# Last 192 tokens of each batch through the second MoE layer with weights and tokens swapped, and the result turned in 32 by 32 blocks on VectorE

## The chip, the cores and the metric

One core of a Trainium2 chip. The metric is the device time of one execution in microseconds (us). Each kernel was run several times beside runs of the kernel before on the same chip, and compared with them. A run of one kernel counts as slow when it takes over 1.5% longer than the fastest run of the same kernel, else as fast. One execution of each was profiled, on a clock that starts with the profile's span; that span is about 2 us shorter than the time of the run. Engines in the profile: PE (TensorE matmul), PEld (weight load), ACT (ScalarE), DVE (VectorE), POOL (GpSimd), SP (SyncE, which here only issues DMAs; "SPq" and "ACTq" lines are issues of DMAs). The granted clock is the share of the full TensorE clock that the profile's clock record shows. Head and tail are the stretches before PE is in full flow (the first 60 us) and after its last matmul; an eviction copies a result out of PSUM, the memory that PE writes.

## The reference

Eight batches of 2496 tokens with 256 channels. A Fourier mixing layer comes first; then each batch goes through one of eight experts, chosen per batch:

```python
def _moe_ref(x, w_gate, w1, w2):          # x: [8, 2496, 256] from the Fourier layer
    ...
    for e in range(E):
        mask = e_idx == e
        h = np.maximum(x[mask] @ w1[e], 0.0)                      # 256 -> 1024
        out[mask] = gate_w[mask, None, None] * (h @ w2[e])        # 1024 -> 256
```

## The kernel before

The kernel declares operations with an estimated cost, dependencies and a virtual time. A greedy list scheduler then emits them once, so that the order on every engine is static.

The chunks of a batch, and the second layer: hidden activations `hs` stand as weights (128 tokens), w2 streams 256 columns, and the result has tokens on partitions, so that a store writes whole rows of 1 KB.

```python
NCH = [(0, 512), (512, 512), (1024, 512), (1536, 512), (2048, 448)]
# ...
for sp in range(2):                                  # two pairs of token tiles per chunk
    for q in range(4):
        def mm(_, ...):
            i = q // 2
            s0 = min((2 * sp + i) * P, nl - P)       # 0, 128, 256 and 320: the last two overlap
            for ft in range(4 * (q % 2), 4 * (q % 2) + 4):
                nc.tensor.matmul(oc["p"][:, i, :], cell["hs"][:, ft, s0 : s0 + P],
                                 w2s_t[b][:, ft, :], start=(ft == 0), stop=(ft == E - 1))
    # ... eviction times the gate, on ACT or DVE, 128 x 512 fp32
    def st(_, ...):
        if 256 * sp + 256 <= nl:
            nc.sync.dma_start(out=out[b, r0 : r0 + 256, :].rearrange("(i p) c -> p i c", p=P), in_=ost)
        else:                                        # last pair: 128 rows and 64 rows
            nc.sync.dma_start(out=out[b, r0 : r0 + P, :], in_=ost[:, 0, :])
            nc.sync.dma_start(out=out[b, r0 + P : ns + nl, :], in_=ost[64:P, 1, :])
```

With 448 tokens the fourth tile computes 64 tokens a second time.

The same sync queue carries the two trips to DRAM of the Fourier layer of the batches that follow. Their names are used throughout:

```python
# A -> fwd ("fwd stores"), four per batch, then fwd -> XB ("XB loads"), five per batch, which feed PE
nc.sync.dma_start(out=fwd_t[b][6 * g0 : 6 * g1].rearrange("(g q) k c -> (q k) g c", q=6),
                  in_=A_t[b][:, g0:g1, :])
nc.sync.dma_start(out=XB_t[b][:, 4 * q : 4 * q + 4], in_=fwd_t[b][:, 4 * q : 4 * q + 4])
# V -> scr ("scratch stores"), five per batch, then scr -> V2 ("V loads"; the profile calls both tiles V)
nc.sync.dma_start(out=scr_t[b][i][:, k : k + 4, :], in_=hc["V"])
nc.sync.dma_start(out=V2_t[b][rows, g0:g1, :], in_=scr[0:126].rearrange("(g q) k c -> (q k) g c", q=6)[:, g0:g1, :])
```

## Time and profile before

| | kernel before |
|---|---|
| time, median (range of 3 runs) | 435.06 us (434.79 to 435.96) |
| span of the profile | 433.1 us |
| PE busy, granted clock | 97%, 1.0 |
| PE's share of the chain that ended last | 89% |
| end of PE, from there to the end of the span | 429.4 us, 3.7 us |

From the page of the kernel before: busy time of the engines (us, share of the span, instructions) and the chain that ended last, by engine and by line.

```profile
PE 419.6 (97%) x3553; PEld 312.2 (72%) x3553; DVE 300.8 (69%) x614; ACT 333.0 (77%) x643; POOL 35.4 (8%) x57
...
PE 89%; DMA 5%; ACT 3%; POOL 1%; SPq 1%; issue 0%; DVE 0%; ACTq 0%; POOLq 0%
PE ps L1300 30%; PE ps L1337 29%; PE ps L895 9%; DMA xin<-in_x_dram 4%; PE ps L1040 4%; PE ps L527 3%; PE ps L793 3%; PE ps L857 3%; PE ps L1219 2%; PE ps L699 2%; ACT hs L1312 1%; DMA tf<-d_tf 1%; PE ps L613 1%; PE ps L732 0%; POOL xin L321 0%
```

L1300 is the first MoE layer and L1337 the second. No load of XB or V is in the chain. The busy share alone would not prove a PE bound, because matmuls overlap in the pipeline; so I also took the distance between the starts of successive matmuls and subtracted the columns' time. Starts are 56 ns apart at 128 columns, 109 at 256, 189 at 448 and 216 at 512, which is columns/2.4 + 2.5 ns. The columns sum to 411.3 us and PE loses 13.6 us to waits, of which 12.1 us in the first 60 us. This sum, "PE's lost time", is used below.

The timeline of the sync queue in one period (start us, duration us, instruction, and how many in a row were merged):

```profile
101.92 0.33 SPq L967 DMA_DIRECT2D V<-scr  x1
102.30 0.74 SPq L972 DMA_DIRECT2D V<-scr  x1
103.54 0.40 SPq L1364 DMA_DIRECT2D out_dram<-ost  x1
104.38 0.36 SPq L1369 DMA_DIRECT2D out_dram<-ost  x1
104.80 0.51 SPq L1371 DMA_DIRECT2D out_dram<-ost  x1
109.77 0.35 SPq L815 DMA_DIRECT2D fwd<-A  x1
...
122.18 2.24 SPq L834 DMA_DIRECT2D XB<-fwd  x5
```

L1369 and L1371 are the two stores that the change replaces. After them the queue is idle for more than 4 us, until the first fwd store at 109.77.

The end of the kernel before, same columns; in brackets idle time before an instruction and what ended it:

```profile
427.30 2.13 PE L1337 MATMUL ps<-w2s,hs 128*128 128x256 f16 x17
...
429.47 0.47 ACT L1378 ACTIVATE ost<-ps,gbc 64x256 f32<-64x256 f32 x1 [1.12 <-PE ps L1337]
429.97 0.55 ACTq L1381 DMA_DIRECT2D out_dram<-ost  x1
```

One eviction and one DMA follow PE's last matmul.

### The profile page before, as it was taken

What the parts mean: (1) busy time and instruction counts of PE and PEld (TensorE: products, weight loads), DVE (VectorE), ACT (ScalarE), POOL (GpSimd) and SP (SyncE); (2) the same over time, 40 slices, a digit from 0 to 9 for tenths busy, and PEclk for the clock granted to TensorE, in tenths of its full rate; (3) what the DMA queues carried; (4) which work ended last, traced back from release to release, by engine and by line L of the source; (5) the groups of instructions that cost most, each with busy time, mean ns of one, the idle gap of its engine ahead of it and who ended that gap; (6) DMA issues with size and microseconds to landing.
All of it is one profiled execution on the core that took longest, in us unless ns stands there. A gap on an engine that the chain in (4) does not pass through costs nothing.

```text
span 433.1 us, 9390 instructions
## 1 busy us (share of the span) xinstructions
PE 419.6 (97%) x3553; PEld 312.2 (72%) x3553; DVE 300.8 (69%) x614; ACT 333.0 (77%) x643; POOL 35.4 (8%) x57
## 2 busy tenths in 40 slices
PE   5888999999999999999999999999999999999996
PEld 2456567778777877778777877778777787777775
DVE  1488866577977787786977878777877869513561
ACT  3789987688876877678867888678777788678884
POOL 5230100011002000021001100020000010000000
PEclk9999999999999999999999999999999999999999
DMA  8899197999895997879995998959987285521122
GB/s 153 224 181 148 33 248 230 200 174 206 208 280 121 226 197 206 248 140 239 180 243 183 194 205 214 284 103 226 207 215 236 87 160 129 182 88 68 50 99 92
DMA packets 85785, 76.96 MB, mean 178 GB/s; under 512 B 7673, under 2 KB 72695, under 8 KB 85740
## 3 DMA queue, kind: packets, MB, share of 16 engines
q1 hardware_dynamic: 68262, 57.41, 48.3%
q0 software_dynamic: 17216, 18.70, 28.5%
q8 instruction: 28, 0.46, 0.5%
q10 hardware_dynamic: 262, 0.25, 0.2%
q14 instruction: 17, 0.14, 0.1%
HBM read 57.54 MB, written 37.49 MB: 219 GB/s over the span
## 4 chain that ended last, share of the span: by engine, by line
PE 89%; DMA 5%; ACT 3%; POOL 1%; SPq 1%; issue 0%; DVE 0%; ACTq 0%; POOLq 0%
PE ps L1300 30%; PE ps L1337 29%; PE ps L895 9%; DMA xin<-in_x_dram 4%; PE ps L1040 4%; PE ps L527 3%; PE ps L793 3%; PE ps L857 3%; PE ps L1219 2%; PE ps L699 2%; ACT hs L1312 1%; DMA tf<-d_tf 1%; PE ps L613 1%; PE ps L732 0%; POOL xin L321 0%
## 5 line engine op out<-in xcount | busy, mean ns | idle before, releaser
L1312 ACT ACTIVATE hs<-ps 128x512 f16<-128x512 f32 (+1 forms) x293 | 168.2, 594 | 68.6 <-PE ps L1300 64.7
L1300 PE MATMUL ps<-ysb,w1s 128*128 128x512 f16 (+1 forms) x640 | 178.4, 374 | 0.1
L1337 PE MATMUL ps<-w2s,hs 128*128 128x256 f16 x1152 | 162.4, 272 | 0.1
L1337 PEld LDWEIGHTS <-hs 128*128 128x128 f16 x1152 | 110.8, 98 | 42.7 <-issue 0.2
L1300 PEld LDWEIGHTS <-w1s 128*128 128x128 f16 x640 | 68.6, 113 | 18.8 <-issue 0.6
L909 DVE TENSOR_TENSOR tt<-ps,bias 128x512 f16<-128x512 f32 x60 | 38.6, 686 | 24.5 <-PE ps L895 24.5
L937 DVE TENSOR_TENSOR Y<-z,cl 64x512 f16<-64x512 f16 x120 | 50.4, 420 | 2.8
L895 PE MATMUL ps<-w,XT 128*128 128x256 f16 x360 | 49.4, 273 | 0.0
L1354 ACT ACTIVATE ost<-ps,gbc 128x512 f32<-128x512 f32 x65 | 44.8, 689 | 2.3 <-PE ps L1337 2.3
L895 PEld LDWEIGHTS <-XT 128*128 128x128 f16 x360 | 35.2, 98 | 7.7
L918 DVE TENSOR_TENSOR z<-ps,tt 128x512 f16<-128x512 f32 x60 | 38.4, 681 | 0.1
L803 ACT CAST A<-ps 120x512 f16<-120x512 f32 x48 | 29.5, 614 | 7.0 <-PE ps L793 6.6
L1056 DVE CAST ysb<-ps 128x468 f16<-128x468 f32 (+1 forms) x24 | 15.0, 629 | 25.6 <-PE ps L1040 25.5
L1056 ACT CAST ysb<-ps 128x468 f16<-128x468 f32 (+1 forms) x60 | 28.0, 523 | 3.2 <-PE ps L1040 2.6
L865 DVE CAST XT<-ps 128x512 f16<-128x512 f32 x24 | 16.5, 688 | 16.0 <-PE ps L857 16.0
L534 ACT CAST V<-ps 128x512 f16<-128x512 f32 x44 | 25.7, 609 | 0.0
L793 PE MATMUL ps<-xin,wa 117*120 117x512 f16 x66 | 23.1, 380 | 0.4 <-ACT ysb L1013 0.4
L534 DVE CAST V<-ps 128x512 f16<-128x512 f32 x26 | 17.9, 688 | 6.5 <-PE ps L527 5.4
L1040 PE MATMUL ps<-wi,V 120*128 120x117 f16 (+1 forms) x308 | 22.4, 214 | 0.0
L865 ACT CAST XT<-ps 128x512 f16<-128x512 f32 x36 | 22.0, 615 | 0.0
L527 PE MATMUL ps<-Y,ti 128*128 128x256 f16 x140 | 21.8, 272 | 0.0
L1040 PEld LDWEIGHTS <-V 120*128 120x128 f16 x308 | 19.8, 98 | 2.4
(104 smaller groups left out, 415.0 us busy)
## 6 DMA issues: line engine op xcount, KB each, us to landing
out_dram<-ost SPq DMA_DIRECT2D x72, 256.0 KB
xin<-in_x_dram POOLq DMA_DIRECT2D x21, 429.0 KB, 11.3
scr<-V SPq DMA_DIRECT2D x35, 256.0 KB
XB<-fwd SPq DMA_DIRECT2D x30, 256.0 KB
V<-scr SPq DMA_DIRECT2D x14, 504.0 KB
fwd<-A SPq DMA_DIRECT2D x18, 360.0 KB
w1s<-in_moe_w_dram POOLq DMA_DIRECT2D x8, 512.0 KB, 7.1
w2s<-in_moe_w_dram POOLq DMA_DIRECT2D x8, 512.0 KB, 8.9
```

What stands on the lines that cost most here:

```text
L534: COPY[eng](out=hc["V"][:, n * u : n * u + n].rearrange("p i c -> p (i c)"), in_=hc["p", u])
L865: COPY[eng](out=cell["X"][:, ch, :, 0:2].rearrange("p a r i k -> p a i r k"), in_=hc["p"].rearrange("p (a i r k) -> p a i r k", a=2, i=2, ...
L895: nc.tensor.matmul(pm[:, D * a : D * a + D], cell["X"][:, ch, a, t].rearrange("p i k -> p (i k)"), w4[:, ch, t, :], start=(ch == 0), stop= ...
L909: nc.vector.tensor_add(out=cell["tt"][:, r], in0=cell["T", 2].rearrange("p (a c) -> p a c", a=2), in1=bias[:, r].unsqueeze(1).to_broadcast ...
L918: nc.vector.tensor_add(out=cell["z"][:, r], in0=cell["T", 1 - r].rearrange("p (a c) -> p a c", a=2), in1=cell["tt"][:, r])
L937: nc.vector.tensor_sub(out=Y[64 * r : 64 * r + 64, :, i], in0=cell["z"][s, r], in1=cell["cl"][s, r])
L1040: nc.tensor.matmul(pi[:, 117 * i : 117 * i + M], V2[:, g, ch * P : ch * P + P], w)
L1056: COPY[eng](out=yv[:, :, 12 * gb : 12 * gb + 3 * nf].rearrange("p a (g j) -> p a g j", j=3), in_=pi[:, 0 : 117 * nf].rearrange("p (g a j) ...
L1300: nc.tensor.matmul(ph[:, 0:nl], w1v[:, ch, fc // 4, :, fc % 4], ysb_t[b][:, ch, ns : ns + nl], start=(ch == 0), stop=(ch == 1))
L1312: nc.scalar.activation(out=o, in_=i, func=AFT.Relu)
L1337: nc.tensor.matmul(oc["p"][:, i, :], cell["hs"][:, ft, s0 : s0 + P], w2s_t[b][:, ft, :], start=(ft == 0), stop=(ft == E - 1))
L1354: nc.scalar.activation(out=ost, in_=oc["p"], func=AFT.Copy, scale=gbc_t[b])
```

## The change

The intent is to stop computing 64 tokens twice. For the last 192 tokens of each batch w2 stands as the weights and the tokens stream (192 columns), twice for the two halves of 128 channels. Channels are then on partitions, so DVE turns the evicted tile in blocks of 32 by 32. After that each row of 32 channels of a token is contiguous, but the blocks of a token lie on four groups of partitions, so eight stores with pieces of 128 bytes put them in place. In the last batch the list order of the two pairs is reversed.

```diff
-    NCH = [(0, 512), (512, 512), (1024, 512), (1536, 512), (2048, 448)]
+    NCH = [(0, 512, ((0, P), (2 * P, 3 * P))), ... ,          # cut
+           (2048, 448, ((0, P), 256))]
+    def add_turned(b, ns, nl, s0, cell, h_ops, hk, wk, gb_op, v):
+        n = nl - s0                                            # 192
+        for h in range(2):
+            def mm(_, h=h):
+                # cut: one PSUM bank, both halves
+                for ft in range(E):
+                    nc.tensor.matmul(
+                        oc["p"][:, h], w2s_t[b][:, ft, P * h : P * h + P],
+                        cell["hs"][:, ft, s0:nl],
+                        start=(ft == 0), stop=(ft == E - 1))
+        # cut: eviction of 128 x 384 times the gate, on ACT or DVE
+        def tr(_):
+            oc["t"] = ot = opool.tile([P, 2, D], FP32, name="ost")
+            nc.vector.transpose(out=ot..., in_=oc["o"]...)     # cut
+        e = S.op("DVE", 0.5, tr, v, deps=[e], lat=0.6)
+        def st(_):
+            ov = out[b, ns + s0 : ns + nl, :].rearrange(
+                "(t r) (h q c) -> q r h t c", r=32, h=2, c=32)
+            for q in range(4):
+                for h in range(2):
+                    nc.sync.dma_start(
+                        out=ov[q, :, h],
+                        in_=ot[32 * q : 32 * q + 32, n * h : n * h + n].rearrange(
+                            "r (t c) -> r t c", c=32))
+        S.op("SP", 2.4, st, v, deps=[e], dma=1.5)
...
-                v = v0 + PERIOD * (c * 8 + fc) / 44
+                v = v0 + PERIOD * (x + fc * nl / 512) / 44     # x = ns / 64
...
+            if b == B - 1 and c == 4:
+                order = order[::-1]
```

More of the change, by code (lines that the diff above doesn't have):

```diff
@@ L1149, in add_gating @@
         return w, o, wk
-    NCH = [(0, 512), (512, 512), (1024, 512), (1536, 512), (2048, 448)]
+    NCH = [(0, 512, ((0, P), (2 * P, 3 * P))), (512, 512, ((0, P), (2 * P, 3 * P))),
+           (1024, 512, ((0, P), (2 * P, 3 * P))), (1536, 512, ((0, P), (2 * P, 3 * P))),
+           (2048, 448, ((0, P), 256))]
     def add_weight_sums(b, w, wk, v):
@@ L1276, with ev @@
     T_t = {}
+    def add_turned(b, ns, nl, s0, cell, h_ops, hk, wk, gb_op, v):
+        n = nl - s0
+        tag = "o" if b < B - 1 else "h"
+        ok = S.tok(tag, BANKS[tag])
+        oc = {}
+        for h in range(2):
+            def mm(_, h=h):
+                if h == 0:
+                    oc["p"] = bank(tag)[:, 0 : 2 * n].rearrange(
+                        "p (h t) -> p h t", h=2)
+                for ft in range(E):
[3 more added lines that the diff above has]
+                        start=(ft == 0), stop=(ft == E - 1))
+            m = S.mm([n] * E, mm, v, deps=h_ops, after=m if h else None,
+                     allocs=[] if h else [ok])
+            hk.rel.append(m)
+            wk.rel.append(m)
+        def ev(eng):
+            oc["o"] = ost = opool.tile([P, 2, D], FP32, name="ost")
+            o = ost.rearrange("p h c -> p (h c)")[:, 0 : 2 * n].rearrange(
+                "p (h t) -> p h t", h=2)
+            if eng == "ACT":
+                nc.scalar.activation(out=o, in_=oc["p"], func=AFT.Copy,
+                                     scale=gbc_t[b])
+            else:
+                nc.vector.tensor_scalar_mul(out=o, in0=oc["p"],
+                                            scalar1=gbc_t[b])
+        e = S.evac(2 * n, ev, v, deps=[m, gb_op])
+        ok.rel.append(e)
+        def tr(_):
+            oc["t"] = ot = opool.tile([P, 2, D], FP32, name="ost")
+            nc.vector.transpose(
+                out=ot.rearrange("p h c -> p (h c)")[:, 0 : 2 * n],
+                in_=oc["o"].rearrange("p h c -> p (h c)")[:, 0 : 2 * n])
+        e = S.op("DVE", 0.5, tr, v, deps=[e], lat=0.6)
+        def st(_):
+            ot = oc["t"].rearrange("p h c -> p (h c)")[:, 0 : 2 * n]
+            ov = out[b, ns + s0 : ns + nl, :].rearrange(
[7 more added lines that the diff above has]
+        S.op("SP", 2.4, st, v, deps=[e], dma=1.5)
     def add_moe(b, y_ops, yk, gate):
@@ L1282, in add_moe @@
             t_op = add_weight_sums(b, w, wk, v0 - 0.05 * PERIOD)
-        for c, (ns, nl) in enumerate(NCH):
+        for c, (ns, nl, tiles) in enumerate(NCH):
+            x = ns / 64
             hk = S.tok("hs", BUFS["hs"])
@@ L1320, in add_moe @@
                 continue
-            for sp in range(2):
+            order = [*enumerate(tiles)]
+            if b == B - 1 and c == 4:
+                order = order[::-1]
+            for sp, tile_s in order:
+                if isinstance(tile_s, int):
+                    add_turned(b, ns, nl, tile_s, cell, h_ops, hk, wk, gb_op,
+                               v0 + PERIOD * (x + 6 * nl / 512 + 4 * sp) / 44)
+                    continue
                 tago = "o" if b < B - 1 else "h"
                 ok = S.tok(tago, BANKS[tago])
-                last = b == B - 1 and c == 4 and sp == 1
+                last = b == B - 1 and c == 4
                 ok2 = S.tok(tago, BANKS[tago])
@@ L1327, in add_moe, with mm @@
                 for q in range(4):
-                    v = v0 + PERIOD * (c * 8 + 6 + 4 * sp + q) / 44
-                    def mm(_, sp=sp, q=q, nl=nl, cell=cell, oc=oc, tag=tago,
+                    if q // 2 >= len(tile_s):
+                        break
+                    v = v0 + PERIOD * (x + 6 * nl / 512 + 4 * sp + q) / 44
+                    def mm(_, tile_s=tile_s, q=q, cell=cell, oc=oc, tag=tago,
                            last=last):
@@ L1334, in mm @@
                         i = q // 2
-                        s0 = min((2 * sp + i) * P, nl - P)
+                        s0 = tile_s[i]
                         for ft in range(4 * (q % 2), 4 * (q % 2) + 4):
@@ L1362, in st @@
                     r0 = ns + 256 * sp
-                    if 256 * sp + 256 <= nl:
-                        nc.sync.dma_start(
-                            out=out[b, r0 : r0 + 256, :].rearrange(
-                                "(i p) c -> p i c", p=P),
-                            in_=ost)
-                    else:
-                        nc.sync.dma_start(out=out[b, r0 : r0 + P, :],
-                                          in_=ost[:, 0, :])
-                        nc.sync.dma_start(out=out[b, r0 + P : ns + nl, :],
-                                          in_=ost[64:P, 1, :])
+                    nc.sync.dma_start(
+                        out=out[b, r0 : r0 + 256, :].rearrange(
+                            "(i p) c -> p i c", p=P),
+                        in_=ost)
                 def ev_last(_, ns=ns, nl=nl, sp=sp, oc=oc):
@@ L1378, in ev_last @@
                     nc.scalar.activation(
-                        out=ost[64:P, 1], in_=oc["p", 1][64:P, 1],
-                        func=AFT.Copy, scale=gbc_t[b][64:P])
-                    nc.scalar.dma_start(out=out[b, r0 + P : ns + nl, :],
-                                        in_=ost[64:P, 1, :])
+                        out=ost[:, 1], in_=oc["p", 1][:, 1],
+                        func=AFT.Copy, scale=gbc_t[b])
+                    nc.scalar.dma_start(out=out[b, r0 + P : r0 + 2 * P, :],
+                                        in_=ost[:, 1, :])
                 def ev_first(_, ns=ns, sp=sp, oc=oc):
```

## The prediction

> What bounds the kernel now. PE is busy 97% of the 433.1 us span at a granted clock of 1.0 (busy shares, clock row) and holds 89% of the chain that ended last; the only DMA in that chain (5%) is at the start. In the trace, matmuls of one line start 109 ns apart at 256 columns, 56 ns at 128, 189 ns at 448, 216 ns at 512. That is columns/2.4 + about 2.5 ns, as the Trainium skill has it (TensorE: Matmul & The Clock Gate, section "Back-to-back issue gap"); this trace agrees. Weight loads (98 ns each) hide even under 128 columns. So the time is a sum of streamed columns plus head and tail; ACT (77%) and DVE (69%) are second.
>
> What the change does. In the 448-token chunk of each batch, the last two 128-token tiles overlapped by 64 tokens: 16 matmuls x 256 columns. Now w2 stands and 192 tokens stream: 16 x 192 columns, estimate 82.5 ns each. Saved: 16 x (109 - 82.5) = 0.42 us per batch, 3.4 us over 8 batches, all on the PE chain. That is the ceiling of the gain, 0.8%.
>
> Added per batch: an eviction of 384 instead of 512 columns (estimate 0.58 us, between the measured 482 ns at 256 and 689 ns at 512), one DVE transpose of 128x384 fp32 (estimate 0.5 us), and 8 stores of 24 KB in 128-byte pieces in place of two stores (0.36 + 0.49 us of issue). Back-to-back issues of small DMAs take about 0.45 us in the trace (XB loads 0.43, 64-row stores 0.47), so 8 take about 3.5 us on SP. In the middle batches SP waited up to 4.2 us just there for the next A tiles, so this should nearly fit. 1536 pieces of 128 bytes per batch: packets of 256 bytes took 18 ns and of 512 bytes 39 ns on average, so 2 to 4 us of the 16 engines per batch. The Trainium skill (DMA: Bandwidth & Descriptors, "Specifications") says writes below 512 B are read-modify-write; no run shows its cost yet. I allow 0 to 2 us for PE waits from this and from the reshuffled static order.
>
> The tail. The instruction order shows that in the last batch, although the tiles are listed in reverse, the scheduler places the turned matmuls last on PE, the transpose last on DVE and its 8 stores last on SP. Before: PE ends at 429.45, ACT eviction 0.47, one store issue 0.55, end at 433.1: 3.65 us after PE. After: eviction 0.58, transpose 0.5, hand-overs 0.1, 8 issues 3.5, landing and end 2.6 (as before from the end of the issue): about 7.3 us after PE. So the tail costs about 3.6 us, off PE but on the critical path, and eats the 3.4 us.
>
> Sum: 435.06 - 3.4 + 3.6 + about 0.7 for waits and the new order = 436.0 us. Range 433.8 to 439.0. Chances: faster by over 2% 0.01, within 2% 0.95, slower by over 2% 0.04.
>
> What would show it. Turned matmuls start 82 to 83 ns apart; PE's last matmul ends 2.5 to 3.5 us earlier than 429.45; from there to the end 6.5 to 8.5 us, with the transpose and eight store issues last; issues of turned stores 0.4 to 0.5 us each; about 12,000 more packets of 128 bytes; the same granted clock.
>
> What would make it wrong. Store issues costing much less (0.3 us: tail only 2 us longer) or much more; 128-byte writes so slow that they delay scratch trips, with PE waits on XB or V loads; a static order luckier or worse by over 1 us; output buffers held long enough to stall ACT.

## More of the kernel before

PE does not wait for them: this is the group of the matmuls that use XB (count, busy us, mean ns of one, idle us before), and what V loads cost the sync queue (us in total, times, longest).

```profile
L857 PE MATMUL ps<-tf,XB 128*128 128x128 f16 x240 | 18.3, 219 | 0.0
...
SPq L1364 <- DMA V<-scr: 3.7, 5, 0.9
```

## The result

| | before | after |
|---|---|---|
| time, median (range, 4 runs each) | 435.37 us (434.79 to 435.96) | 447.74 us (446.42 to 449.99) |
| ratio, 95% interval | | 1.0289 (1.0243 to 1.0336) |
| span of the profile | 433.1 us | 448.3 us |
| PE busy, granted clock | 97%, 1.0 | 94%, 0.986 |
| time of all columns on PE | 411.3 us | 407.9 us |
| PE's lost time between 100 and 340 us | 0.9 us | 14.4 us |
| from PE's end to the end of the span | 3.7 us | 7.4 us |

A ratio is the mean time of one kernel's fast runs over the mean of the other's in the same rounds, so it is not quite the ratio of the medians. The result is slower by 2.9%, outside the stated range.

From the page after, the same lines as before:

```profile
PE 422.2 (94%) x3553; PEld 311.7 (70%) x3553; DVE 303.1 (68%) x626; ACT 336.7 (75%) x639; POOL 35.1 (8%) x57
...
PE 78%; DMA 12%; ACT 4%; SPq 1%; issue 1%; POOL 1%; DVE 1%; ACTq 0%; POOLq 0%
PE ps L1356 26%; PE ps L1402 23%; PE ps L895 8%; DMA XB<-fwd 5%; DMA xin<-in_x_dram 4%; PE ps L793 3%; PE ps L1040 3%; PE ps L527 3%; PE ps L857 3%; PE ps L1221 3%; DMA scr<-V 2%; PE ps L1292 2%; PE ps L699 2%; ACT hs L1368 1%; DMA tf<-d_tf 1%
```

The chain now leaves PE for XB loads and scratch stores, 7% of the span together. Two lines of the view of waits after (who waited for whom: us in total, times, longest) name the engine that lost the time, and one line of the sync queue's own waits says what held the turned stores (L1327):

```profile
PEld L857 <- DMA XB<-fwd: 10.9, 5, 3.4
...
PE ps L857 <- DMA XB<-fwd: 8.5, 5, 3.0
```

```profile
SPq L1327 <- DMA V<-scr: 21.5, 6, 4.7
```

The turned stores write results that no V load touches, and still they waited for V loads, once in each of six batches. The records of each issue in the trace explain it: this program gives the sync queue's DMAs eight completion semaphores in rotation, and a DMA first waits until the DMA that used its semaphore eight issues earlier has landed. Two V loads and six turned stores use up the eight; the seventh and the eighth turned store must wait for the V loads. The timeline of the sync queue after, in the period shown above:

```profile
106.18 0.34 SPq L972 DMA_DIRECT2D V<-scr  x1
106.62 7.22 SPq L1327 DMA_DIRECT2D out_dram<-ost  x8
113.95 1.45 SPq L815 DMA_DIRECT2D fwd<-A  x1
115.49 0.44 SPq L546 DMA_DIRECT2D scr<-V  x1
116.02 1.42 SPq L815 DMA_DIRECT2D fwd<-A  x1
...
121.16 2.15 SPq L815 DMA_DIRECT2D fwd<-A  x1
...
126.42 2.24 SPq L834 DMA_DIRECT2D XB<-fwd  x5
```

The eight stores hold the queue for 7.2 us, of which 3.4 us is that wait (the view of waits limited to this stretch) and the rest eight issues of 0.44 us (their median). The first fwd store goes out at 113.95, 4.2 us later than before, and the XB loads at 126.42, also 4.2 us later. PE waits at 131.15 and again in each of the four following periods. In one of them the wait was long enough to cost clock as well. The longest wait of the timeline after, and the same kernel's busy times by stretch (stretch, length, engines' busy time, PEclk, DMA share, GB/s):

```profile
184.38 1.03 PE L857 MATMUL ps<-tf,XB 128*128 128x128 f16 x8 [2.96 <-DMA XB<-fwd]
```

```profile
183.00:191.00 8.00, 6.62 (x34) 4.47 (x35) 2.40 (x4) 1.62 (x3) 0.00 (x0) 0.57 0.74 251
```

The clock record has PE at half clock from 183.55 to 190.38 us, 6.8 us. The Trainium skill (TensorE: Matmul & The Clock Gate, "What's actually happening") describes half rate after an idle window of about 3.4 us. Here the wait was 3.0 us on PE and 3.4 us on the weight load, but the record turned to half 0.8 us before it ended, 2.6 us after the last weight load; so the trace agrees that a long wait costs clock, but not on the length. The matmuls that then ran at half clock (256 columns 213 ns apart instead of 109) cost 2.9 us of the 14.4 us. Of the four timed runs, two had a mean granted clock of 0.986 and 0.987 and took 448.3 to 450.0 us; the other two had 0.993 and 0.994 and took 446.4 to 447.1 us. The loss is there without the dip in the clock, so the dip is a consequence and the smaller part.

The turned matmuls and the transpose themselves, from the groups by line and shape (count, busy us, mean ns of one, idle before):

```profile
L1292 PE MATMUL ps<-hs,w2s 128*128 128x192 f16 x128 | 12.9, 246 | 0.0
L1316 DVE STREAM_TRANSPOSE ost<-ost 128x384 f32<-128x384 f32 x8 | 4.6, 578 | 13.4 <-ACT ost L1306 13.4
```

The mean of 246 ns is the length of one pipelined matmul; the starts of the turned matmuls are 82 ns apart. The end of the kernel after:

```profile
439.44 1.48 PE L1292 MATMUL ps<-hs,w2s 128*128 128x192 f16 x16
439.69 0.47 ACT L1437 ACTIVATE ost<-ps,gbc 128x256 f32<-128x256 f32 x1 [2.04 <-PE ps L1402]
...
440.96 0.58 ACT L1306 ACTIVATE ost<-ps,gbc 128x384 f32<-128x384 f32 x1 [0.80 <-PE ps L1292]
441.57 0.58 DVE L1316 STREAM_TRANSPOSE ost<-ost 128x384 f32<-128x384 f32 x1 [2.26 <-ACT ost L1306]
442.18 3.90 SPq L1327 DMA_DIRECT2D out_dram<-ost  x8
```

The sum over both profiles: columns -3.4 us, PE's lost time in the middle +13.5, in the last 90 us +0.6, in the head +0.9 (the head varies by about that much between any two profiles), the tail +3.7: together +15.3 us, against 15.2 us measured between these two spans.

### The profile page after: what moved, and what is told of

Same layout as the page of the kernel before. It is cut to its first block, busy times and chain, and to the rows that moved or that the text cites. A ratio compares the mean times of both kernels' runs of the same rounds, so it can differ in the third digit from the quotient of the medians.

```text
span 448.3 us, 9474 instructions
## 1 busy us (share of the span) xinstructions
PE 422.2 (94%) x3553; PEld 311.7 (70%) x3553; DVE 303.1 (68%) x626; ACT 336.7 (75%) x639; POOL 35.1 (8%) x57
## 4 chain that ended last, share of the span: by engine, by line
PE 78%; DMA 12%; ACT 4%; SPq 1%; issue 1%; POOL 1%; DVE 1%; ACTq 0%; POOLq 0%
PE ps L1356 26%; PE ps L1402 23%; PE ps L895 8%; DMA XB<-fwd 5%; DMA xin<-in_x_dram 4%; PE ps L793 3%; PE ps L1040 3%; PE ps L527 3%; PE ps L857 3%; PE ps L1221 3%; DMA scr<-V 2%; PE ps L1292 2%; PE ps L699 2%; ACT hs L1368 1%; DMA tf<-d_tf 1%
## 5 line engine op out<-in xcount | busy, mean ns | idle before, releaser
L1368 ACT ACTIVATE hs<-ps 128x512 f16<-128x512 f32 (+1 forms) x306 | 175.0, 590 | 70.7 <-PE ps L1356 66.7
L1402 PE MATMUL ps<-w2s,hs 128*128 128x256 f16 x1024 | 147.0, 274 | 0.0
L1402 PEld LDWEIGHTS <-hs 128*128 128x128 f16 x1024 | 99.9, 98 | 41.9 <-issue 2.3
L1419 ACT ACTIVATE ost<-ps,gbc 128x512 f32<-128x512 f32 x52 | 35.6, 685 | 0.9 <-ACT ysb L1056 0.7
L1056 DVE CAST ysb<-ps 128x468 f16<-128x468 f32 (+1 forms) x36 | 21.2, 592 | 20.7 <-PE ps L1040 19.8
L534 ACT CAST V<-ps 128x512 f16<-128x512 f32 x53 | 30.6, 599 | 0.5
L857 PE MATMUL ps<-tf,XB 128*128 128x128 f16 x240 | 19.8, 222 | 8.5 <-DMA XB<-fwd 8.5
L803 ACT CAST A<-ps 120x512 f16<-120x512 f32 x43 | 24.3, 617 | 2.8 <-PE ps L793 2.8
L857 PEld LDWEIGHTS <-XB 128*128 128x128 f16 x240 | 15.8, 99 | 14.0 <-DMA XB<-fwd 10.9
L1056 ACT CAST ysb<-ps 128x468 f16<-128x468 f32 (+1 forms) x48 | 21.9, 529 | 1.8 <-PE ps L1040 1.8
```

Of the source, the lines that this page charges most:

```text
L857: nc.tensor.matmul(px[:, P * i : P * i + P], XB_t[b][:, k1, ch * P : ch * P + P], tf[:, k1, :])
L1056: COPY[eng](out=yv[:, :, 12 * gb : 12 * gb + 3 * nf].rearrange("p a (g j) -> p a g j", j=3), in_=pi[:, 0 : 117 * nf].rearrange("p (g a j) ...
L1368: nc.scalar.activation(out=o, in_=i, func=AFT.Relu)
```

## The experiments

Theory A: the sync queue is held too long by the eight stores (their issues, and the landing wait eight DMAs back), so fwd stores and XB loads come late and PE waits. Theory B: the 1536 pieces of 128 bytes per batch load the DMA engines. Theory C: the rearranged static order costs the time. Later a theory D, that the turned work itself is needed for the loss.

In the first four runs only the emission of the stores was changed, not what the scheduler was told: the order on PE, ACT, DVE and POOL is identical to the changed kernel's (compared instruction by instruction), and on SP identical but for the stores themselves.

### e1_eight_long: eight stores, long pieces

```diff
-  ov = out[b, ns+s0 : ns+nl, :].rearrange("(t r) (h q c) -> q r h t c", r=32, h=2, c=32)
+  ov = out[b, ns+s0 : ns+nl, :].rearrange("n c -> (n c)").rearrange("(q h r e) -> q h r e", q=4, h=2, r=32)
```

> The changed kernel with its 8 turned stores per batch, same bytes, but each writes 32 contiguous pieces of 768 bytes instead of 192 pieces of 128 bytes (the result is wrong on purpose). Order of instructions on all five engines is identical to the changed kernel's. Theory A (the sync queue is held: 8 issues in a row, and issues 7 and 8 wait until the two V loads issued 8 DMAs earlier have landed, so the fwd stores and XB loads behind them come late and PE waits for XB): stays slow, 444 to 449 us. Theory B (1536 pieces of 128 bytes per batch load the DMA engines): falls to 432 to 436 us. Theory C (the rearranged static order itself): 447 us.

Measured: 442.89 us, ratio 1.0173 (1.0136 to 1.0209). Its output is wrong, which doesn't matter for the time. PE's lost time in the middle is still 10.3 us. Most of the loss stays without any short piece, so B is not the main cause. The time is lower than the 444 to 449 us expected for A, though, so short pieces do add to the hold: from the first store to the first fwd store it lasts 7.2 us here and 8.4 us in the changed kernel (means of five periods). By the medians against the kernel before, 8.0 us of the loss of 12.4 us stay and 4.4 us go with the short pieces. The wait of the stores for V loads is as long without them (22.2 us, 7 times).

### e2_one_short and e3_one_long: one store

```diff
-  for q in range(4):
-      for h in range(2):
-          nc.sync.dma_start(...)                       # 8 stores
+  nc.sync.dma_start(out=flat.rearrange("(j p c) -> p j c", p=P, c=32), in_=ot.rearrange("p (j c) -> p j c", c=32))   # e2: 1536 pieces of 128 bytes
+  nc.sync.dma_start(out=flat.rearrange("(p e) -> p e", p=P), in_=ot)                                                # e3: 128 pieces of 1536 bytes
```

> One store per batch of the same bytes in the same 1536 pieces of 128 bytes (wrong result on purpose), same order on all engines otherwise. Theory A: the queue is held for about 0.4 us only; PE no longer waits for XB and the tail shrinks from 7.4 to about 4.5 us: 432 to 435 us. Theory B: stays at 445 to 449 us. Theory C: 447 us.

> One store per batch in 128 pieces of 1536 bytes (wrong result on purpose), same order otherwise. Theories A and B both: about 432 us, that is before minus 3.4 us of PE plus 0.5 us of longer tail. Theory C (order): 445 us or more. The difference of this run to the one-store run with short pieces is the cost of 128-byte pieces alone.

Measured: 434.40 us, ratio 0.9989 (0.9958 to 1.0019), for one store in 128-byte pieces; 433.84 us, ratio 0.9966 (0.9931 to 1.0001), for one store in long pieces. Their outputs are wrong, which doesn't matter for the times. The loss is gone with all the matmuls, transposes and short pieces still in place, so B and C fall as main causes. Between the two runs short pieces cost 0.6 us when the queue is not held, which is not clear of noise (the intervals overlap); the tail in the two profiles is 5.1 us with them and 4.2 us without. C keeps a small part: in both, PE's lost time in the middle is 1.9 us instead of 0.9 and in the last 90 us 1.2 instead of 0.6, with no wait for XB.

### e4_swap: V loads behind the turned stores

```diff
   def rd(_, i=i, k0=k0, k9=k9, g0=g0, g1=g1):        # emits a V load
+      if i == 0 and b >= 2:
+          HOLD.append(lambda: rd_now(...)); return    # first pair of V loads: kept back
...
   # in st(), after the eight turned stores
+  for f in HOLD: f()
+  HOLD.clear()
```

> The changed kernel (right result) with one swap on the sync queue in six batches: the two V loads that stood just ahead of the 8 turned stores now stand just behind them, so no turned store has a V load 8 DMAs ahead of it. Theory A with the landing wait as its main part: the hold falls from about 7.2 to 3.6 us and the time to 436 to 441 us. Theory A with the 8 issues as its main part: 444 us or more. Theories B and C: 447 us.

Measured: 436.41 us, ratio 1.0039 (1.0008 to 1.0070), right result. Eight stores with 128-byte pieces remain; only two DMAs changed places with them, and nearly 11 of the 12.4 us are gone. The timeline of the sync queue of this kernel, in the same period:

```profile
102.57 4.22 SPq L1334 DMA_DIRECT2D out_dram<-ost  x8
107.75 0.31 SPq L974 DMA_DIRECT2D V<-scr  x1
108.11 0.56 SPq L979 DMA_DIRECT2D V<-scr  x1
108.78 0.37 SPq L816 DMA_DIRECT2D fwd<-A  x1
...
122.43 2.24 SPq L835 DMA_DIRECT2D XB<-fwd  x5
```

The hold is 4.2 us instead of 7.2, it starts earlier because the stores no longer stand behind the V loads' own wait for scratch, and the fwd store is on time again. PE ends at 427.0 us, 2.4 us before the kernel before; the tail of 7.3 us takes that back. The swap removes two things at once, the landing wait and the place behind the V loads. Run e5 below tests the second.

### d1_behind and d2_ahead: tiny stores in the kernel before

```diff
+  def small_stores(b):
+      for i in range(6):                                       # 1 KB each, to a DRAM tile of their own
+          nc.sync.dma_start(out=d_i, in_=eye[0:16, 0:32])
   # d1: called just after the first pair of V loads of a batch; d2: just ahead of it
```

> The kernel before, nothing turned, with six tiny stores of 1 KB put on the sync queue just behind each pair of V loads (six batches), so that the seventh and eighth DMA after the loads must wait for them as the last two turned stores did. Order on all other engines identical to the kernel before. Theory A (the landing wait, 8 DMAs back, in the sync queue's order is what costs): 441 to 447 us, with PE waiting for XB loads and sync waits on V loads of about 20 us. Rival (the number of issues in a row, or the 128-byte data): at most 1 us over the control with the stores ahead.

> Control: the same six tiny stores per batch put just ahead of the V loads. Same number of issues. Both theories: 435 to 437 us.

Measured: 435.84 us, ratio 1.0013 (0.9988 to 1.0038), behind; 434.92 us, ratio 0.9998 (0.9976 to 1.0021), ahead. The expectation for the stores behind was a miss. The landing wait did appear (in the view of waits the sync queue waited 24.4 us for V loads, 12.6 and 11.8 us on two lines, against 3.7 us in the kernel before), but PE lost nothing. The timeline says why: the hold began at 103.75 and ended with the first fwd store at 111.05, only 1.3 us later than in the kernel before, since the queue's idle time stood at that place. So the landing wait by itself is harmless at this place. What counts must be how late the fwd stores leave; in the changed kernel the stores also began 3 us later, at 106.6. The sync queue of d1_behind in that period ("idle" is the tile that the tiny stores write):

```profile
103.75 3.02 SPq L492 DMA_DIRECT2D idle<-eye  x6
109.47 0.40 SPq L1371 DMA_DIRECT2D out_dram<-ost  x1
...
111.05 0.57 SPq L820 DMA_DIRECT2D fwd<-A  x1
```

### d3_hold12 and d3_hold20: longer holds in the kernel before

```diff
   nc.sync.dma_start(out=out[b, r0 + P : ns + nl, :], in_=ost[64:P, 1, :])
+  if b < 6: small_stores(b)                                    # 12 or 20 tiny stores
```

> The tiny stores behind the V loads did not slow the kernel before: there the sync queue's hold reached only to 111.05 us (first fwd store of that period, against 109.77 before and 113.95 in the changed kernel), because 4.1 us of idle queue time soaked it up. Theory A in its threshold form: the time is lost only once the hold outlasts that idle time by more than the slack of the fwd-XB-PE trip. This run: kernel before, 12 tiny stores (about 5 us) put where the turned stores stood, just ahead of the first fwd store, in six batches; same order on all other engines. Theory A: fwd about 1 us late, 435 to 437 us.

> As before with 20 tiny stores (about 8.4 us of hold, first fwd store at about 114 us as in the changed kernel). Theory A in threshold form (only the length of the hold counts, whatever fills it): 440 to 447 us, with PE waiting for XB. Rival D (it takes the turned work itself: its order, its data or its transpose): within 2 us of the kernel before.

Measured: 454.46 us (448.27 to 458.36), ratio 1.0478 (1.0428 to 1.0529), with 12, where two of the four runs count as slow and are in these figures (the two fast ones, 448.27 and 452.31 us, are 3.1 and 4.1% above the median of the kernel before); 476.77 us, ratio 1.0967 (1.0938 to 1.0996), with 20. Both results are right; the expected sizes were too small. Each tiny store also waits for the landing of the DMA eight issues earlier, V loads and other tiny stores among them, so twelve held the queue until 117.0 and twenty until 120.1 us instead of the 110.8 and 114 I had worked out. The direction and the victim are as A says. With 20 tiny stores, the sync queue in the first period, and from the view of waits (L862 is L857 of the kernel before):

```profile
106.04 13.95 SPq L492 DMA_DIRECT2D idle<-eye  x20
120.11 0.36 SPq L820 DMA_DIRECT2D fwd<-A  x1
...
PE ps L862 <- DMA XB<-fwd: 31.6, 5, 7.4
```

Nothing is turned here, every other engine has the order of the kernel before, and PE waits for XB as in the changed kernel. Theory D falls. With the runs so far, in the first period that is affected:

| run | first fwd store at | first XB load at | PE's lost time, 100 to 340 us |
|---|---|---|---|
| e4_swap | 108.8 us | 122.4 us | 2.0 us |
| e5_four_noswap | 109.1 | 123.8 | 1.9 |
| before | 109.8 | 122.2 | 0.9 |
| d1_behind | 111.1 | 123.0 | 0.9 |
| e1_eight_long | 112.5 | 124.7 | 10.3 |
| after | 114.0 | 126.4 | 14.4 (2.9 of it half clock) |
| d3_hold12 (its fastest run) | 117.0 | 128.3 | 12.6 (to 350 us, to take in its fifth wait) |
| d3_hold20 | 120.1 | 131.3 | 34.7 (without its fifth wait, at 369 us) |

In this period a fwd store about 1.3 us late costs nothing, and one 2.8 us late or more costs time. These times also carry the head, which differs by up to 2.4 us between profiles; a measure without it is the lead, from the first fwd store to the moment when PE is ready for XB (the start of its first matmul on XB less the wait before it). In the kernel before it is 19.1 us in all five periods. Over the runs of this table and f1_swap_tail, PE never waited with a lead of 17.3 us or more, and waited 1.1 to 7.6 us in each of the 20 periods with a lead of 15.6 us or less (after, e1, d3); no period lies between. So at least 1.8 us of lateness are free.

### f1_swap_tail: the last batch left alone

```diff
+  if b == B - 1 and c == 4:
+      tiles = (tiles[0], (2 * P, nl - P))                      # two overlapping tiles, as before
```

> The swapped version with the last batch left as it was before (two overlapping tiles, no transpose), right result. If the tail is what is left of the loss, as predicted: 3.6 us of tail back, 0.42 us of PE given up, so about 433.2 us, 0.4 percent under before. If the tail were covered by something else: 436 us.

Measured: 434.13 us, ratio 0.9978 (0.9956 to 1.0001), right result. The tail is back to 3.6 us. The time is 0.9 us above the expected 433.2 us.

### f2_four: four stores of 256-byte pieces

```diff
-  oc["p"][:, h], w2s_t[b][:, ft, P * h : P * h + P], ...       # channels of one half
+  oc["p"][:, h], w2s_t[b][:, ft, h : D : 2], ...               # every second channel
-  nc.vector.transpose(out=flat, in_=flat)
+  nc.vector.transpose(out=flat.rearrange("p (t c h) -> p h t c", c=32, h=2), in_=...)
-  8 stores, "(t r) (h q c) -> q r h t c"
+  4 stores, "(t r) (q e) -> q r t e", pieces of 64 channels
```

> As the swap-and-tail version, with four stores of 48 KB in 256-byte pieces per batch instead of eight of 24 KB: the stationary columns are every second channel, and the transpose writes the two halves interleaved. Right result. Halves the hold of the sync queue and the pieces. If the queue's hold still costs PE anything after the swap: 432.0 to 432.8 us; if not: the same as the swap-and-tail version within 0.4 us.

Measured: 434.03 us, ratio 0.9968 (0.9947 to 0.9989), right result. It equals f1_swap_tail, so once the swap is made the length of the hold costs nothing more. This is the first version with a right result whose interval lies wholly under the kernel before: 0.3% faster, far inside the 2% under which two kernels count as the same.

### e5_four_noswap: four stores, V loads where the change had them

```diff
-      if i == 0 and b >= 2:
-          HOLD.append(...); return                             # the swap taken out of f2_four
```

> Four stores of 256-byte pieces per batch, last batch as before, but the V loads left ahead of the stores, as the changed kernel has them. Right result. Theory A: four issues take 1.8 us and none of them has a V load 8 DMAs ahead, so it equals the four-store version with the swap: 433.5 to 435 us. If the swap mattered by something else than the hold (the V loads being early, the stores standing behind the loads' own wait for scratch): 437 us or more.

Measured: 433.96 us, ratio 0.9975 (0.9955 to 0.9996), right result. The stores begin at 106.8 us, behind the V loads and as late as in the changed kernel, but four issues end at 109.0 and the fwd store leaves at 109.1. So standing behind the V loads is harmless as well when the hold is short. The loss of the change comes from both together: a late start, and eight DMAs in a row that run into the landing wait. How much is the eight issues and how much the landing wait was not isolated: no run has eight stores that start late without that wait. Its share rests on the record of waits (3.4 of 7.2 us). Without it the first fwd store would leave at about 110.5 us (an estimate, 113.95 less 3.4), a lateness that cost nothing in d1_behind.

### f3b_order: an order nearer to before

```diff
-  v = v0 + PERIOD * (x + fc * nl / 512) / 44
+  v = v0 + PERIOD * (c * 8 + fc) / 44                          # and the same for the second layer, in f2_four
```

> The four-store version with the swap, with the virtual times of the MoE work set as in the kernel before instead of scaled by the chunk length, so that the PE order is nearer to that of before (928 rows differ instead of 1504). PE's sum of waits in the four-store version is 1.6 us above before's although its columns are 3 us fewer; if that comes from the rearranged order, this run may give back up to 1.5 us: 432.5 to 434 us; if not, 434 us.

Measured: 434.33 us, ratio 0.9984 (0.9964 to 1.0003), right result. No gain: PE's lost time in the middle rose to 3.2 us. That the order costs the 1.6 us is so not shown by this run, and which order would give them back stays open.

## Why the prediction was wrong

- **PE saves 3.4 us: right.** The turned matmuls start 82 ns apart (82.5 predicted), and the columns sum to 407.9 instead of 411.3 us.
- **Eviction, transpose, tail: right.** Eviction 0.58 us and transpose 0.58 us (0.58 and 0.5 predicted); eight issues at the end 3.9 us (3.5 predicted); from PE's end to the end 7.4 us (7.3 predicted). f1_swap_tail, which left the last batch alone, brought the tail back to 3.6 us.
- **Packets: right in number.** 12,288 packets of 128 bytes were added. Their own cost, measured by one store with and without short pieces, is 0.6 us, not clear of noise. In eight stores they cost more, since they lengthen the hold: 4.4 of the 12.4 us of loss go when only the pieces are made long (e1).
- **The step that failed: "In the middle batches SP waited up to 4.2 us just there for the next A tiles, so this should nearly fit", with 8 issues at "about 3.5 us on SP".** The issue time of 0.44 us each was right, but the hold was 7.0 to 10.1 us in the five periods. I took the queue's time as the sum of issue times and overlooked that a DMA also waits for the landing of the one eight issues earlier, here a V load; the wait was 3.4 us in the period shown and 21.5 us in total. Nor did I see that in the new order the stores begin later (106.62 against 104.38 us for the two that they replace), behind V loads that themselves wait for scratch. The hold outlasted the idle time, the XB loads left 4 us late, and PE lost 13.5 us more in the middle than before (9.4 us of waits for XB, 2.9 us of half clock, and 1.2 us of small waits that the turned versions without waits for XB have too) where I had allowed 0 to 2 us. The runs with tiny stores (d1, d3) show that it is the lateness of the fwd stores that counts.
- **"the reshuffled static order": right as a small term.** PE's lost time is 1.6 to 1.8 us higher in the turned versions without waits for XB (2.0 and 1.3 us in f1_swap_tail, against 0.9 and 0.6 before). I put it down to the order by elimination; the trace has it in small waits of up to 0.17 us near the same places in each period, but f3b_order did not give it back. That is most of why the repaired versions gain 0.7 to 1.4 us (by their ratios), not 3.
- **What would make it wrong: named in part.** I listed delayed scratch trips with PE waits on XB, but put them down to slow 128-byte writes. One store with the same pieces (e2) has no such waits, and eight stores with long pieces (e1) keep most of them; so the pieces are about a third of the loss, by way of a longer hold, and not its main cause.

## What to carry to other kernels

Before putting several small DMAs on a queue that also feeds the bottleneck, count what stands as many issues ahead of them as the queue has completion semaphores (eight here): a queue's time is issue times plus landing waits, and the next transfer pays for both. Compare the sum with the idle time of the queue at that very place and with the slack of the transfer behind it; in this kernel a hold under that threshold cost nothing, and over it the loss came back every period. When a change saves matmul columns by giving results a worse layout for storing, choose the layout so that few stores suffice: here every second channel as weights gave four stores instead of eight, and with the last batch left as it was a loss of 2.9% became a gain of 0.3%. Not tried: the stores on another queue, or a program with more completion semaphores.

## What the Trainium skill lacked or had wrong

- DMA: Bandwidth & Descriptors, "Why a DMA increments its semaphore by 16 and not by 1", advises one semaphore per slot in flight, and does not say what a small rotating set costs. With the eight of this program the turned stores waited 21.5 us in six batches for V loads that they have nothing to do with.
- No page says what lengthens an issue on the sync queue. The fwd stores took 0.43 us to issue on average in the kernel before and 1.28 us in the changed kernel (25 issues each, from 98 us on), but also 1.20 us in e2_one_short, where the queue was not late; the cause stays open.
- DMA: Bandwidth & Descriptors, "Specifications", says that transfers under 512 bytes are read-modify-write. No run here shows that mechanism; 12,288 pieces of 128 bytes cost 0.6 us in all when the queue was not held, and their packets took 13 ns (median). In eight stores that held the queue they cost 4.4 us.
- TensorE: Matmul & The Clock Gate, "Back-to-back issue gap", gives about 81 ns at 128 columns and 131 ns at 512 for streams with weight loads. Here such streams ran at 56 and 216 ns, which is the page's formula for an isolated matmul.
